# An interleaved two-layer decode kernel: w_down in 6272-byte runs, gate and up columns with a step of seven, the FFN result read once, new instruction orders

## The chip, the cores and the metric

One core of a Trainium2 chip. The metric is the device time of one execution in microseconds: 278.97 us, the median of three runs (278.21 to 281.98). TensorE (PE; its weight loads are PEld), VectorE (DVE), ScalarE (ACT) and GpSimd (POOL) compute; SyncE (SP) issues the transfers.

## What is computed

Four tokens (B = 4), each with a row x of 448 numbers, go through the same two blocks twice: attention over the last 2048 keys of a cache, and a gated FFN.

```python
x = A_x
x = x + _A_ref(_layernorm(x), ...)   # attention
x = x + _B_ref(_layernorm(x), ...)   # FFN
x = x + _A_ref(_layernorm(x), ...)   # the same weights and caches again
x = x + _B_ref(_layernorm(x), ...)

def _B_ref(x, w_gate, w_up, w_down):       # 448x1792, 448x1792, 1792x448
    g = _silu(x @ w_gate)
    return (g * (x @ w_up)) @ w_down
```

Attention has 16 query heads on 8 K/V heads of 256, bf16. K and V of the window are 64 MB for all tokens and heads in one layer; with weights and with what is loaded again for the second layer, some 96 MB are moved.

## The kernel before

**Tokens and heads.** A head of one token and layer is written t, layer, head: 301 is token 3, layer 0, head 1. `PLAN` lists the pairs of heads that are worked as one group, in 27 steps; a token's layer 1 (112, 113 and so on) is mixed with layer 0 of the next token. PLAN isn't changed.

**K and V slots.** Each K or V half (512 KB, 4096 bytes on each of 128 partitions) goes into one of 31 slots of the tile `half` (7 more are free once wq is done with). Part of a token's K and V stays for layer 1. SP issues the loads in the order `SEQ_SP`, with the slots of `SLOTS`; a load into a used slot waits for the matmul that read it last, and everything behind it in the queue waits too.

**A group.** DVE transposes each K half in place (L982, in blocks of 32). PE makes scores S (L1016), DVE the maximum (L1031), PE spreads it (L1036, L1039), DVE reduces again (L1045), ACT the exponent (L1049), PE turns the probabilities (L1060), ACT copies them (L1068), PE sums (L1076) and multiplies with V (L1090), DVE and POOL make the reciprocal (L1081, L1103), ACT and DVE take the result (L1105, L1107), PE flips it (L1113), DVE scales it (L1123), and PE projects it with wo into bank A, as rows (L1143) or columns (L1135).

**The FFN of a token in layer 0.** `rows` (L883 to L897) turns what is in rows; `residual` makes xn, the bf16 column form, early (L875), and xr in fp32 (L903). `norm` makes the odd part xe (L589, L592), the sums (L596, L599 with PE L602, DVE L609), and on POOL the inverse root (L615 to L625). Since the FFN starts ahead of the norm, the mean is put in afterwards with a matmul of the columns' sums (L629, L816). Gate and up are 14 x 4 matmuls each (L801): a 128x128 piece of the weights is loaded, and a column of xn, repeated to 32, streams through. Gate is in bank Z, up in bank Z2. ACT makes tanh (L832), DVE two products (L835, L846), then 56 matmuls with w_down (L853) put the result into bank Z again. That is for tokens 1 to 3; token 0's FFN comes after its mean is taken off (L607), and leaves the columns' sums (L843). In layer 1 there is one FFN for all four tokens at the end, with 8 columns for each.

**After it.** Three DVE operations (L870) read bank Z: `xn` (bf16, for the q projection), `xr` (fp32, for the norm), `xs` (fp32, kept for layer 1). Each is z * scale + old value. Then a norm (L589 to L623), the q projection (L683, into banks Z and Z2; it writes bank Z first, so it waits until Z was read), ACT and DVE copies (L694, L691), a turn (L703) with `tmean` (L665), L710, L717, L722, and the factor for the scores, `rid` (L650).

**The weights of the FFN.** Chunk fc of the hidden row has features 128 fc to 128 fc + 127. `w[:, cc * FF + fc * 128 : ... + 128]` is the piece for rows 128 cc of gate or up; the last 64 rows of w are folded into 128 partitions, half of the columns in each, so that chunk fc lies at (fc % 7) * 128 there. w_down is loaded (L576) with partition p of chunk c holding row 128 c + p, in rows of 896 bytes.

**Orders.** Every operation has a number, in the order in which the program makes them. `SEQ_PE`, `SEQ_DVE`, `SEQ_ACT`, `SEQ_POOL` and `SEQ_SP` say in which order each engine runs them. An engine runs in order, and waits at an operation for semaphores of other engines. `w` in `SEQ_PE` is a filler: a matmul of 128x128 by 512 that adds zero to bank A (L1253), to keep PE busy; there are 223. `HELD` says which fillers may come before a read of bank A.

Of the kernel before, what the change touches and what calls it, by code (L numbers as in the profile page):

```python
# [6 lines left out]
ALU = mybir.AluOpType  # L7
# [43 lines left out]
ROWF = ()  # L51
# [35 lines left out]
).split()  # L87
SEQ_DVE = (
# [18 lines left out]
).split()  # L107
SEQ_ACT = (
# [5 lines left out]
).split()  # L114
SEQ_POOL = (
# [8 lines left out]
).split()  # L124
SEQ_SP = (
# [13 lines left out]
).split()  # L139
HELD = (  # L140
    "0 44 44 44 94 94 99 99 115 115 119 122 139 139 145 145 195 195 201 201 208 208 213 213 215 215 215 215 215 215 "
    "215 215"
).split()
MMV = 0.034
FAR = 1e30
# [1184 lines left out]
```

## Time and profile before

| | |
|---|---|
| Runs | 278.97, 278.21, 281.98 us |
| The profiled execution | 279.5 us, its span from the first to the last instruction 277.7 |
| TensorE's mean granted clock | 0.969 |
| Busy | PE 209.0 us, weight loads 125.0, DVE 173.8, POOL 76.5, ACT 47.3 |
| Transfers | 96.68 MB, mean 348 GB/s, in 28474 packets, 6928 of them under 2 KB |
| FFN matmuls | 560 for gate and up, 280 for w_down |

A busy PE isn't PE at its peak, since matmuls are pipelined. In the chain of waits each piece is what the following one waited for. In a timeline a row is: start and length in us, engine, line, operation, tiles, count, and in brackets the idle time before it and what ended it. In a row of windows: the stretch, its length, busy us (and number of instructions) of PE, PEld, DVE, ACT and POOL, the granted clock, the busy share of the DMA engines (it can exceed 1), and GB/s.

### The profile page before, as it was taken

The page shows a single profiled execution, that of the slowest core. Times are in us where ns is not written, and L with a number is a line of the kernel's source. Part 1 is how long each engine was busy: PE and PEld are TensorE (multiplying, and loading weights), DVE is VectorE, ACT ScalarE, POOL GpSimd, SP SyncE. Part 2 cuts the span into 40 slices and gives each one's busy share as a digit, 9 for nine tenths or more (in the row PEclk, how much of TensorE's full clock was granted, in tenths as well). Part 3 has the DMA queues.
Part 4 walks back from the last instruction along what each step waited for, and adds up shares of the span by engine and source line. Part 5 has one row for each costly group of instructions (what it writes and reads, how often), then busy time and mean ns, then how long its engine had stood idle before and what let it go on. Part 6 is the DMA issues. An engine that isn't in the chain of part 4 may idle for free.

```text
span 277.7 us, 9966 instructions
## 1 busy us (share of the span) xinstructions
PE 209.0 (75%) x4424; PEld 125.0 (45%) x4424; DVE 173.8 (63%) x522; ACT 47.3 (17%) x115; POOL 76.5 (28%) x195
## 2 busy tenths in 40 slices
PE   0000076699788968988998897899699798899997
PEld 0000032355464634455754444474454356456694
DVE  7973056445545799368447995655789845559751
ACT  0000000232111220121113221211022031032510
POOL 1000017142204412421253342124132332043650
PEclk9999999999989999999999999999979999599998
DMA  7999999999999999999799999939999999589200
GB/s 292 394 419 412 403 412 406 402 396 401 389 379 405 357 396 415 407 409 353 260 332 410 409 405 411 405 150 362 362 417 407 410 408 346 215 279 408 79 5 1
DMA packets 28474, 96.68 MB, mean 348 GB/s; under 512 B 2828, under 2 KB 6928, under 8 KB 27792
## 3 DMA queue, kind: packets, MB, share of 16 engines
q1 hardware_dynamic: 28423, 96.06, 88.8%
q8 instruction: 34, 0.56, 0.8%
q14 instruction: 9, 0.07, 0.1%
q10 hardware_dynamic: 8, 0.00, 0.0%
HBM read 96.05 MB, written 0.00 MB: 346 GB/s over the span
## 4 chain that ended last, share of the span: by engine, by line
PE 43%; DMA 25%; DVE 13%; SPq 10%; issue 4%; ACT 3%; POOL 2%; ACTq 0%
DMA half<-in_A_k_cache_dram 16%; PE A L1253 10%; DMA half<-in_A_v_cache_dram 9%; PE S L1016 8%; DVE half L982 7%; PE Y L1090 6%; SPq L992 5%; PE Z L801 4%; SPq L976 3%; PE Z L683 3%; SPq L558 2%; PE Z L853 2%; PE A L1143 2%; PE Y L1060 2%; PE A L1135 2%
## 5 line engine op out<-in xcount | busy, mean ns | idle before, releaser
L982 DVE STREAM_TRANSPOSE half<-half 128x1024 uint32<-128x1024 uint32 x80 | 97.2, 1231 | 22.3 <-DMA half<-in_A_k_cache_dram 22.2
L1253 PE MATMUL A<-identb,small 128*128 128x512 bf16 x223 | 67.4, 404 | 0.3 <-DVE xr L903 0.3
L1103 POOL TENSOR_TENSOR small<-small 128x4 f32<-128x4 f32 x32 | 32.5, 1017 | 70.1 <-DVE small L1081 64.7
L1090 PE MATMUL Y<-half,pT 128*8 128x256 bf16 x1024 | 38.7, 275 | 3.2 <-issue 1.4
L1016 PE MATMUL S<-half,qe 128*8 128x256 bf16 (+1 forms) x1120 | 35.3, 269 | 6.3 <-issue 2.0
L1016 PEld LDWEIGHTS S<-half,qe 128*8 128x8 bf16 x1120 | 24.4, 84 | 16.2 <-issue 3.8
L1023 POOL TENSOR_TENSOR qe<-qc,small 128x64 bf16<-128x64 bf16 x56 | 15.3, 295 | 47.6 <-PE S L1016 33.9
L921 PE MATMUL Z<-identb,wo_sb 4*128 4x4 bf16 x4 | 0.3, 167 | 36.7 <-DMA wo_sb<-in_A_x_dram 36.7
L1031 DVE TENSOR_REDUCE small<-S 104x1 bf16<-104x256 f32 x32 | 13.4, 417 | 22.0 <-PE S L1016 22.0
L1090 PEld LDWEIGHTS Y<-half,pT 128*8 128x8 bf16 x1024 | 21.3, 85 | 12.0 <-DVE small L1081 3.2
L1253 PEld LDWEIGHTS A<-identb,small 128*128 128x128 bf16 x223 | 19.1, 103 | 14.9 <-issue 6.4
L1105 ACT ACTIVATE oh<-Y 128x256 bf16<-128x256 f32 x32 | 12.2, 383 | 36.2 <-PE Y L1090 27.2
L615 POOL TENSOR_SCALAR st<-st 128x1 f32<-128x1 f32 x16 | 4.5, 280 | 50.1 <-DVE st L609 50.1
L1107 DVE SCALAR_TENSOR_TENSOR oh<-oh,small,Y 128x256 bf16<-128x256 bf16 x32 | 15.0, 469 | 4.0 <-ACT oh L1105 3.8
L921 PEld LDWEIGHTS Z<-identb,wo_sb 4*128 4x128 bf16 x4 | 0.2, 104 | 36.6 <-DMA wo_sb<-in_A_x_dram 36.6
L1143 PE MATMUL A<-wo_sb,oT 128*4 128x448 bf16 x200 | 13.8, 352 | 1.3 <-DVE oT L1123 1.3
L1049 ACT ACTIVATE praw<-S,small 104x256 bf16<-104x256 f32 x16 | 7.6, 472 | 38.9 <-DVE small L1045 38.9
L1049 ACT ACTIVATE praw<-S,small,st 104x256 bf16<-104x256 f32 x16 | 9.0, 564 | 30.1 <-DVE small L1045 26.6
L1068 ACT ACTIVATE pT<-Y 128x192 bf16<-128x192 f32 x32 | 10.5, 329 | 15.5 <-PE Y L1060 14.1
L683 PE MATMUL Z<-half,small 128*5 128x512 bf16 x160 | 10.9, 379 | 1.5 <-DVE small L592 1.4
L1081 DVE TENSOR_REDUCE small<-Y 128x4 f32<-128x64 f32 x32 | 6.7, 213 | 7.8 <-PE Y L1076 7.6
L1060 PE MATMUL Y<-selt,praw 104*64 104x48 bf16 x256 | 10.1, 197 | 1.8 <-ACT praw L1049 1.7
(135 smaller groups left out, 245.8 us busy)
## 6 DMA issues: line engine op xcount, KB each, us to landing
half<-in_A_v_cache_dram SPq DMA_DIRECT2D x80, 512.0 KB, 13.5
half<-in_A_k_cache_dram SPq DMA_DIRECT2D x76, 512.0 KB, 10.7
wo_sb<-in_A_wo_dram SPq DMA_DIRECT2D x8, 448.0 KB, 11.8
half<-in_A_wq_dram SPq DMA_DIRECT2D x3, 1024.0 KB, 16.2
half<-in_A_k_cache_dram SPq DMA_DIRECT2D x2, 1024.0 KB, 6.4
wd_sb<-in_B_w_down_dram SPq DMA_DIRECT2D x1, 1568.0 KB, 18.5
wu_sb<-in_B_w_up_dram SPq DMA_DIRECT2D x1, 1344.0 KB, 11.8
wg_sb<-in_B_w_gate_dram SPq DMA_DIRECT2D x1, 1344.0 KB, 14.7
```

What stands on the lines that cost most here:

```text
L683: last = e.matmul(zb[32 * j:32 * j + B + 1, 0:512], lhsT=lhsT, rhs=wq_sb[:, c:c + 512], start=(cc == 0), stop=(cc == 3), skip_group_check= ...
L982: return e.transpose(a, a)
L992: g.dma(pp + VLAG, 1 << 19, lambda e, cell=cell, hv=hv, vsrc=vsrc: e.dma_start(unit(cell), vsrc[hv]), None, w=(f"v{t}_{kvh}_{hv}",), run=4 ...
L1016: last = e.matmul(Sb[s_][qd:qd + 8, c0:c0 + rhs.free_size()], lhsT=qe[q_][:, P, ce, :, :].rearrange("p a n -> p (a n)"), rhs=rhs, start=(c ...
L1023: g.op(*((DVE, 0.13) if layer and fresh.get(t, gi) == gi else (POOL, 0.25)), pos - SLEAD - 1, lambda e, P=P, t=t, kvh=kvh: e.tensor_tensor ...
L1049: return e.activation(praw[0:R, 0:128 * n].rearrange("p (g r l) -> p g r l", g=2 * n, l=2), Sb[s_][0:R, 0:128 * n].rearrange("p (l g r) -> ...
L1060: last = e.matmul(Yb[p_][64 * h:64 * h + 64, c0:c0 + (48 if n == 2 else 32)], lhsT=praw[0:R, 64 * gg:64 * gg + 64], rhs=w, start=(gg == 0) ...
L1090: last = e.matmul(Yb[p_][32 * gg:32 * gg + M, 256:512], lhsT=pT[pt][:, gg, 2 * a + hv, 4 * P:4 * P + M] if n == 2 else p1[:, gg % 2, 2 * a ...
L1103: g.op(POOL, 0.69, pos, lambda e: e.tensor_tensor(ri[p_][:, 0:2 * n], rs[p_][:, 0:2 * n], expo[:, 1:1 + 2 * n], op=ALU.pow), r=(f"rs{p_}", ...
L1107: g.op(DVE, 0.43, pos, lambda e: e.scalar_tensor_tensor(out=oh[:, :], in0=oh[:, :], scalar=lomask[:, 0:1], in1=Yb[p_][:, 256:512], op0=ALU ...
L1143: last = e.matmul(Ab[32 * k:32 * k + B, 0:D], lhsT=oT[oi][:, k % 2, k // 2, :], rhs=wo_sb[:, 4 * kvh + k, :], start=False, stop=False, ski ...
L1253: return e.matmul(Ab[:, 0:512], lhsT=zero[:, 0:1].broadcast_to([128, 128]), rhs=identb[:, :].unsqueeze(1).broadcast_to([128, 4, 128]), sta ...
```

## The change

**w_down.** Chunk fc = 7 h + j now has at partition p the feature 896 h + 7 p + j. Seven rows that follow each other lie in one partition, so a run is 7 x 896 = 6272 bytes, and two of them fill a partition. The gate and up pieces must yield the features in the same order: their 128 columns are every seventh one.

```diff
-            load(rank_d, 1605632, wd_sb[:, :, :], B_w_down.rearrange("(c p) n -> p c n", p=128), "wd", 430)
+            load(rank_d, 1605632, wd_sb[:, :, :].rearrange("p (h j) n -> p h (j n)", h=2),
+                 B_w_down.rearrange("(h p j) n -> p h (j n)", h=2, j=7), "wd", 6272)
...
                         if cc < 3:
-                            lhsT, x = w[:, cc * FF + fc * 128:cc * FF + fc * 128 + 128], xn[:, cc, sl]
+                            c, x = cc * FF + fc // 7 * 896 + fc % 7, xn[:, cc, sl]
                         else:
-                            lhsT = w[:, 3 * FF + (fc % 7) * 128:3 * FF + (fc % 7) * 128 + 128]
-                            x = xe[:, fc // 7, sl]
+                            c, x = 3 * FF + fc % 7, xe[:, fc // 7, sl]
+                        lhsT = w[:, c:c + 890:7]
```

**The FFN result.** One DVE operation reads bank Z and leaves z * scale in `st[:, t, 4:8]`. DVE adds it to xr for xn; POOL adds it to xr and to xs.

```diff
-            for dst, src, key, put in ((xn[:, :, t], xr[:, t, :], f"x{t}", f"xn{t}"), (xr[:, t, :], xr[:, t, :], f"x{t}", f"x{t}"),
-                                       (xs[:, t, :], xs[:, t, :], f"xs{t}", f"xs{t}")):
-                vec(rank, lambda e, dst=dst, src=src: e.scalar_tensor_tensor(
-                    out=dst, in0=zv[:, 0, :], scalar=st[:, t, 14:15], in1=src, op0=ALU.mult, op1=ALU.add),
-                    ("z", f"st{t}t", key), (put,), 0.1, ("Z",))
+            sk, d = f"st{t}", st[:, t, 4:8]
+            vec(rank, lambda e: e.tensor_single_scalar(d, zv[:, 0, :], st[:, t, 14:15], op=ALU.mult),
+                ("z", sk + "t"), (sk + "w", sk + "h"), 0.16, ("Z",))
+            vec(rank, lambda e: e.tensor_tensor(xn[:, :, t], xr[:, t, :], d, op=ALU.add), (f"x{t}", sk + "w"), (f"xn{t}",), 0.14)
+            for a, key in ((xr, f"x{t}"), (xs, f"xs{t}")):
+                g.op(POOL, 0.27, rank, lambda e, a=a: e.tensor_tensor(a[:, t, :], a[:, t, :], d, op=ALU.add),
+                     r=(key, sk + "w"), w=(key,))
```

The first two columns of `st[:, t, 4:8]` are scratch of the norm too, so the norm's L596 waits until POOL has read it.

**Orders.** All five orders, `SLOTS` and `HELD` are new. Each FFN of layer 0 has one operation more, so numbers from 304 on are up by one to four: an operation n of before is n + 1 after token 0's FFN, n + 2 after token 1's, n + 3 after token 2's and n + 4 after token 3's. There are 245 fillers. Two places, with the numbers as each version has them:

```diff
 SEQ_SP, around w_down (117; 115 and 113 are up and gate, 335 and 337 K 101, 437 K 102, 604 is K 200 and becomes 606)
-115 113 335 337 117 437 333 334 340 339
+115 113 338 336 606 117 335 334 341 340
 SEQ_DVE, the end of token 0's FFN (296 L846, 438 the transpose of K 102, 351 L1081, 301 to 303 L870; now 301 the read, 302 xn)
-296 344 346 438 303 351 301 302
+296 352 301 302
 SEQ_DVE, token 3's FFN (1263 and 1265 transposes of K 210, 1269 and 1271 of K 211; 1150 L875, 1151 L903, 1154 L596, 1153 L592, 1155 L599, 1157 L609, 1162 L629, 1174 L835, 1175 L846)
-1150 1151 1154 1153 1155 1157 1162 1271 1174 1269 1263 1265 1175
+1269 1153 1154 1157 1158 1156 1267 1160 1273 1165 1275 1177 1178
 SEQ_PE, token 1 after w_down (579 L589, 590 to 595 L683, 583 L602, 664 value products)
-579 590 591 583 592 664 594 595
+581 592 666 593 585 594
 SEQ_PE, token 3 (1163 to 1171 L801, 1167 and 1172 L816, 1156 L602, 1231 to 1234 value products of group 111, 1276 scores of 210 and 211, 1176 to 1179 L853)
-1231 1165 1168 1169 1166 1167 1232 1233 1170 1171 1172 w w w w w w 1276 1176 1177
+1166 1155 1167 1168 1169 1159 1237 w w w w w 1171 1172 1173 1174 1170 1175 1280 1179
```

The function `ffn_row`, and the branches that call it, are taken out; `ROWF` was empty and PLAN has no step of that kind, so nothing ran there.

More of the change, by code (lines that the diff above doesn't have):

```diff
@@ L50 @@
 DSTART = 2.1
-ROWF = ()
 COLX = {(3, 1): 2}
@@ L135 @@
     "0 1 2 3 4 5 6 7 8 9 10 11 12 13 14 15 16 17 18 19 20 21 22 23 24 25 26 27 28 29 30 3 4 19 21 22 14 20 9 7 10 21 "
[3 rows of a table removed]
[3 rows of a table added]
 ).split()
 HELD = (
-    "0 44 44 44 94 94 99 99 115 115 119 122 139 139 145 145 195 195 201 201 208 208 213 213 215 215 215 215 215 215 "
-    "215 215"
+    "0 45 45 45 110 110 113 113 131 131 133 133 151 151 160 160 220 220 224 224 231 231 237 237 237 237 237 237 237 "
+    "237 237 237"
 ).split()
@@ L724, in qproj @@
                     ("z2",), tuple(f"qc{t}_{h}" for h in range(HKV)), 0.18, ("Z2",))
-        def ffn_row(ts, rank):
-            rowvec(rvec[:, 1:2], "rvf", ts, rank)
-            g.op(POOL, 0.27, rank, lambda e: e.tensor_single_scalar(rvec[:, 2:3], rvec[:, 1:2], 0.5, op=ALU.mult),
-                 r=("rvf",), w=("rvs",))
-            g.op(POOL, 0.27, rank, lambda e: e.tensor_scalar(rvec[:, 3:4], rvec[:, 1:2], rvec[:, 2:3], None, op0=ALU.mult),
-                 r=("rvf", "rvs"), w=("rvt",))
-            def gu(e, gi, c0, c1):
-                last = None
-                w, zb = (wg_sb, wu_sb)[gi], (Zb, Z2)[gi]
-                for cc in range(c0, c1):
-                    for j in range(4):
-                        f0, f1 = 512 * j, min(512 * j + 512, FF)
-                        if cc < 3:
-                            parts = [(xn[:, cc, 0:B], cc * FF + f0, 0, f1 - f0)]
-                        else:
-                            parts = []
-                            for h in range(2):
-                                a, b = max(f0, 896 * h), min(f1, 896 * h + 896)
-                                if a < b:
-                                    parts.append((xe[:, h, 0:B], 3 * FF + a - 896 * h, a - f0, b - a))
-                        for lhsT, c, o, m in parts:
-                            last = e.matmul(zb[32 * j:32 * j + B, o:o + m], lhsT=lhsT, rhs=w[:, c:c + m],
-                                            start=(cc == 0), stop=(cc == 3), skip_group_check=True)
-                return last
-            for gi, (z, bank, w) in enumerate((("z", "Z", "wg"), ("z2", "Z2", "wu"))):
-                g.op(PE, 1.28, rank, lambda e, gi=gi: gu(e, gi, 0, 3), r=XN[0:B] + (w + "a",), w=(z,), bank=(bank,))
-                g.op(PE, 0.5, rank, lambda e, gi=gi: gu(e, gi, 3, 4), r=XE[0:B] + (w + "b",), acc=(z,), bank=(bank,))
-            g.op(SCA, 0.65, rank, lambda e: e.activation(wide[:, :], Zb[:, :], ACT.Tanh, scale=rvec[:, 2:3]),
-                 r=("z", "rvs"), w=WIDE, bank=("Z",))
-            vec(rank, lambda e: e.scalar_tensor_tensor(out=wide[:, :], in0=wide[:, :], scalar=1.0, in1=Zb[:, :],
-                                                       op0=ALU.add, op1=ALU.mult), ("z",), WIDE, 0.65, ("Z",))
-            vec(rank, lambda e: e.scalar_tensor_tensor(out=wideb[:, 0:512], in0=wide[:, :], scalar=rvec[:, 3:4], in1=Z2[:, :],
-                                                       op0=ALU.mult, op1=ALU.mult), ("z2", "rvt"), WIDE, 0.65, ("Z2",))
-            def turn(e):
-                last = None
-                for c in range(4):
-                    last = e.matmul(Zb[:, 16 * c:16 * c + 16].rearrange("p (j t) -> p j t", j=4),
-                                    lhsT=wideb[:, 128 * c:128 * c + 128], rhs=idt, start=(c == 0), stop=True,
-                                    skip_group_check=True)
-                return last
-            g.op(PE, 0.12, rank, turn, r=WIDE + ("identb",), w=("z",), bank=("Z",))
-            vec(rank, lambda e: e.tensor_copy(hT[:, :], Zb[:, 0:64]), ("z",), ("wb",), 0.13, ("Z",))
-            def down(e):
-                last = None
-                for c in range(4):
-                    for j in range(4):
-                        if 4 * j + c < NFC:
-                            last = e.matmul(Ab[32 * j:32 * j + B, 0:D], lhsT=hT[:, 16 * c + 4 * j:16 * c + 4 * j + 4],
-                                            rhs=wd_sb[:, 4 * j + c, :], start=False, stop=False, skip_group_check=True)
-                return last
-            g.op(PE, 1.5, rank, down, r=("wb", "wd"), acc=tuple(f"row{t}" for t in ts), bank=("A",))
@@ L1163, in build @@
             where = {}
-            if not heads:
-                g.tag = ("f", waiting[-1])
-                ffn_row(waiting, pos)
-                for u in waiting:
-                    rows(u, pos)
-                    residual(u, pos)
-                    final(u, pos)
-                g.tag = None
-                waiting = []
-                continue
             for batch in heads:
@@ L1222, in build @@
                 pos = pos_ - CROSS
-                with_ = []
-                rowf = t in ROWF and layer == 0
                 late = (t, layer) in LATE or layer == 1 and t in fin
                 residual(t, pos, late)
-                norm(t, pos, xr, None if rowf or (layer and not late) else fin.index(t) if layer else -1, late)
+                norm(t, pos, xr, None if layer and not late else fin.index(t) if layer else -1, late)
                 if layer == 0:
-                    if rowf:
-                        ffn_row(with_ + [t], pos)
-                        for u in with_ + [t]:
-                            rows(u, pos)
-                            residual(u, pos, u == t and t in QLATE)
-                        for u in with_:
-                            final(u, pos)
-                    else:
-                        ffn(with_ + [t], pos, late, False)
+                    ffn([t], pos, late, False)
                     norm(t, pos, xr, late=t in QLATE)
```

128 rows, old and new, of tables (SEQ_ACT, SEQ_DVE, SEQ_PE, SEQ_POOL) are left out of this document.

## Prediction

> **What bounds the kernel now.** I read the page first, then the chain of waits in order of time, then equal windows of the span, and last the timeline around each token's FFN.
>
> ```profile
> span 277.7 us, 9966 instructions
> ...
> GB/s 292 394 419 412 403 412 406 402 396 401 389 379 405 357 396 415 407 409 353 260 332 410 409 405 411 405 150 362 362 417 407 410 408 346 215 279 408 79 5 1
> ...
> PE 43%; DMA 25%; DVE 13%; SPq 10%; issue 4%; ACT 3%; POOL 2%; ACTq 0%
> ```
>
> Each of the 40 slices is 6.9 us. The loads run at about 405 GB/s for the first 85 us, and fall into four holes: slices 14, 19 to 21, 27 to 29 and 34 to 36. The last three each sit on the FFN of a token. The chain in order of time says the same from the other side:
>
> ```profile
> 64.60 18.34 DMA half<-in_A_k_cache_dram
> ...
> 95.00 12.57 DMA half<-in_A_k_cache_dram
> ...
> 238.82 2.56 PE A L1253 x6
> 241.38 1.44 PE S L1016 x29
> ```
>
> So the first 107 us are bound by the transfers, and the later part by what TensorE, VectorE and the slots do around an FFN: while an FFN runs, no K or V slot comes free, and the queue stands. The last FFN hole is the dearest:
>
> ```profile
> 235.00:240.00 5.00, 4.23 (x90) 2.58 (x87) 4.40 (x6) 0.27 (x1) 1.01 (x3) 0.54 0.65 210
> 240.00:245.00 5.00, 5.00 (x104) 2.92 (x102) 1.14 (x7) 0.61 (x2) 0.00 (x0) 0.77 0.53 197
> 245.00:250.00 5.00, 4.39 (x91) 2.28 (x90) 2.89 (x16) 1.81 (x4) 2.94 (x8) 1.00 0.93 320
> ```
>
> The last number is GB/s, the third from the end the granted clock. Against 410 GB/s these 15 us lack (200 + 213 + 90) x 5 us = 2.5 MB, or 6.1 us.
>
> **Part 1: w_down in long runs.** Transfers of 896-byte rows become 6272-byte runs.
>
> ```profile
> 70.00:74.00 4.00, 2.57 (x61) 1.48 (x59) 1.92 (x9) 0.93 (x2) 0.22 (x2) 1.00 1.03 408
> 75.00:79.00 4.00, 3.49 (x117) 3.22 (x116) 3.02 (x7) 0.27 (x1) 1.42 (x4) 0.57 1.09 347
> ...
> wd_sb<-in_B_w_down_dram SPq DMA_DIRECT2D x1, 1568.0 KB, 18.5
> ...
> 81.71 1.22 PE L853 MATMUL Z<-wide,wd_sb 128*128 128x32 bf16 x42 [0.52 <-DMA wd_sb<-in_B_w_down_dram]
> ```
>
> The down projection of token 0 waits for w_down until 81.7 us, so the window from 75 to 79 is mostly w_down, and the one from 70 to 74 is the gate matrix and K. 1568 KB are 1.606 MB: 4.63 us at 347 GB/s, 3.94 us at 408. That is 0.7 us of transfer time less. Ends: 0 if the time is lost again in the hole at 90 us, 1.0 us if the window still holds some long runs (estimate). [...]
>
> The queue is also reordered: one K half for token 2 (op 604, 512 KB, 1.28 us at 408 GB/s) now goes ahead of w_down. So w_down lands at 81.7 - 0.7 + 1.3 = 82.3. What follows it for token 0:
>
> ```profile
> 82.97 1.25 DVE L982 STREAM_TRANSPOSE half<-half 128x1024 uint32<-128x1024 uint32 x1 [1.55 <-DMA half<-in_A_k_cache_dram]
> 84.14 0.18 DVE L870 SCALAR_TENSOR_TENSOR xs<-Z,st,xs 128x4 f32<-128x4 f32 x1
> 84.37 0.21 DVE L870 SCALAR_TENSOR_TENSOR small<-Z,st,xr 128x4 bf16<-128x4 f32 x1
> 84.61 0.22 DVE L870 SCALAR_TENSOR_TENSOR xr<-Z,st,xr 128x4 f32<-128x4 f32 x1
> 84.89 0.39 PEld L683 LDWEIGHTS Z<-half,small 128*5 128x5 bf16 x12
> ```
>
> Before, a K transpose (op 438) stood on VectorE ahead of the three reads of bank Z, and held them until 84.14; the new order has it later. Now: 56 matmuls at 1.22 / 42 = 29 ns, with about 0.3 us of another group's turn between (estimate), end at 82.3 + 1.9 = 84.2; one read to 84.42, the bf16 row to 84.6, q projection at about 84.65 instead of 84.89. That gain of 0.25 us and the 0.7 us of transfers belong to the same chain (it goes back into the queue at 93 us and out by DMA at 95). I take 0.5 us for both.
>
> **Part 2: the FFN result read once.** Three VectorE operations that read bank Z become one read, one add on VectorE for bf16 xn, and two adds on GpSimd (xs first, then xr). Token 1 in the profile:
>
> ```profile
> 137.86 0.23 DVE L870 SCALAR_TENSOR_TENSOR small<-Z,st,xr 128x4 bf16<-128x4 f32 x1 [1.80 <-PE Z L853]
> 138.00 0.22 DVE L870 SCALAR_TENSOR_TENSOR xs<-Z,st,xs 128x4 f32<-128x4 f32 x1
> 138.13 0.22 DVE L870 SCALAR_TENSOR_TENSOR xr<-Z,st,xr 128x4 f32<-128x4 f32 x1
> 138.41 0.82 PE L683 MATMUL Z<-half,small 128*5 128x512 bf16 x12
> 139.16 0.38 PE L602 MATMUL Z<-st,small 128*128 128x2 f32 x2
> 139.58 0.16 DVE L609 COPY st<-Z 128x2 f32<-128x2 f32 x1 [0.79 <-PE Z L602]
> 139.84 0.30 POOL L615 TENSOR_SCALAR st<-st 128x1 f32<-128x1 f32 x1 [0.25 <-DVE st L609]
> 140.87 0.26 PE L703 MATMUL Z<-small,wide 128*128 128x4 bf16 x4
> ...
> L1245 POOL TENSOR_SCALAR xr<-xr,st 128x4 f32<-128x4 f32 x4 | 1.2, 311 | 7.4 <-DVE st L599 7.4
> ```
>
> The q projection overwrites bank Z, so it waited for all three reads (ending 138.35). Now: read to 138.08, xn 0.16 (as L609's) to 138.24, start near 138.29, 0.12 earlier. The norm goes the other way: its sums need xr, which was there at 138.35. GpSimd starts 0.10 after VectorE's end (139.74 to 139.84), takes 0.31 twice, and VectorE gets it 0.10 later, at 138.90: 0.5 us late. The norm's matmul L602 stands in TensorE's order in the middle of the q projection. For tokens 0 and 2 the new order puts more of it (and value products) ahead of L602, which covers the 0.5; for tokens 1 and 3 only 0.2 us more is put ahead, so TensorE stands some 0.3 us, and all behind L602 with it. Two new waits: GpSimd's adds wait for the read, and behind them stand the reciprocal of another group or the norm's own steps, which aren't due earlier; L596 waits on VectorE for the adds, and behind it stand the norm's steps, at token 2 also the softmax sum of group 301 (L1081), 0.5 us late at most. L703 (140.87) needs what follows L609, whose end goes from 139.74 to 140.24; that leaves 0.6 us for the one VectorE step between. Sum: token 0 counted above, token 1 +0.3, token 2 -0.2 (as token 1's start), token 3 +0.3, with ends of -0.25 and +0.5 for each of the three. I take +0.1 for tokens 1 and 2, and token 3 goes into part 4.
>
> **Part 3: columns with a step of seven.** 560 weight loads (112 for each of five FFNs, half of them the x280 below) read 128 columns 14 bytes apart.
>
> ```profile
> 75.63 1.30 PE L801 MATMUL Z<-small,wu_sb 128*128 128x32 bf16 x42
> ...
> 129.03 1.22 PE L801 MATMUL Z<-small,wg_sb 128*128 128x32 bf16 x42 [0.26 <-DVE small L875]
> ...
> L801 PE MATMUL Z<-small,wg_sb 128*128 128x32 bf16 x280 | 9.0, 180 | 0.3 <-DVE small L875 0.3
> ...
> L703 PE MATMUL Z<-small,wide 128*128 128x4 bf16 x32 | 2.0, 170 | 0.1
> ```
>
> Taking off one matmul's 0.18 us, 42 come every 25 ns at clock 1 and every 27 ns in the window with 0.57. Halving the clock hardly shows, so at the full clock the array's own share is at most 14 ns, and 25 ns is the interval of issue. Reads twice as slow would still fit (2 ns x 112 = 0.25 us per FFN). The nearest stepped weights, L703 with columns 4 bytes apart, come at (0.26 - 0.17) / 3 = 30 ns, like the plain ones. I take 0; the other end is the rival below.
>
> **Part 4: the orders.** PLAN is unchanged, so every group comes in the same place; what moves is the fine order. The largest move is at token 3:
>
> ```profile
> 178.12 1.46 PE L1253 MATMUL A<-identb,small 128*128 128x512 bf16 x6
> ...
> 232.83 0.17 DVE L875 TENSOR_TENSOR small<-xr,A 128x4 bf16<-128x4 f32 x1 [1.00 <-PE A L1135]
> 234.20 0.16 DVE L609 COPY st<-Z 128x2 f32<-128x2 f32 x1 [0.59 <-PE Z L602]
> 234.39 0.24 DVE L629 TENSOR_SCALAR wide<-colsum,st 128x28 bf16<-128x28 f32 x1
> 234.54 1.24 DVE L982 STREAM_TRANSPOSE half<-half 128x1024 uint32<-128x1024 uint32 x1
> 236.39 0.17 DVE L835 SCALAR_TENSOR_TENSOR wide<-wide,Z 128x14 f32<-128x14 f32 x1 [0.60 <-ACT wide L832]
> 236.47 3.49 DVE L982 STREAM_TRANSPOSE half<-half 128x1024 uint32<-128x1024 uint32 x3
> 239.88 0.13 DVE L846 TENSOR_TENSOR wide<-wide,Z 128x14 bf16<-128x14 f32 x1
> ```
>
> Three transposes stood between L835 and L846, and the scores of K 210 and 211 waited for them behind six fillers, 8.3 us after L875 ended (233.0 to 241.3). The new order puts one transpose ahead of L875, where TensorE's output projection runs anyway (1.00 us of idle time, so 0.25 is uncovered), and the others between L599, L609, L629 and L835. Counted from L875: VectorE four small steps like L875's 0.17, three transposes of 1.23, L609 0.16, L629 0.24, together 4.8 us; TensorE 112 x 25 ns = 2.8, the norm's matmul 0.38, 16 value products at the same interval 0.4, and five fillers. One filler takes (1.46 - 0.38) / 5 = 0.216 us, the six less the tail of the last, taken as L602's 0.38; five make 1.1, together 4.7. Scores start at 233.0 + 0.25 + 4.8 = 238.0 instead of 241.3, 3.3 us earlier; less 0.3 for L602, 3.0. Ends: 0 and 3.6. The loads that end the hole wait for these scores, so I carry it to the end.
>
> 22 fillers are added (223 to 245 in the orders). They stand mostly between token 0's late groups and before token 3's FFN. I take 0, since TensorE waits there for K and V; with the cover gone it is 22 x 0.216 = 4.8 us, and the six at 238.82 show that it can be gone.
>
> Sum: 279.5 us for the profiled execution (277.7 of span and 1.8 around it), less 0.5, plus 0.1, less 3.0: 276.1. The median of the runs shown is 0.5 below that execution: 275.5.
>
> **The rivals.** *The hole after token 3 closes (272.4).* Two value products of group 111 now come before and amid gate and up, which frees V slots earlier; if the queue never stands, 6.1 us of missing transfers come back in place of 3.0, and 3.1 less is 272.4. For it: the clock was 0.54 and 0.77 in those windows, and fillers there took 2.56 us for six; a busier TensorE may keep it at 1. Against: the loads behind still wait for the scores of 211.
>
> *The wait is only replaced (278.5).* VectorE works in order. If K 210 has not landed by 233 us, the transposes put ahead of L875 and L609 hold up the norm itself, and 3.0 goes back. For it: K is what the chain waits on elsewhere. Against: at 234.54 and 236.47 no transpose waited for a landing.
>
> *Stepped weight loads become the bound (288.8).* If reading 14 bytes apart takes the array four times as long, 14 ns become 55, 30 more than the issue interval: 112 x 30 = 3.3 us per FFN, four of them on the chain (token 0's has w_down's landing for cover): +13.3. It decides from a factor of about three. Nothing in the trace steps so far; L703's 4 bytes speak against. [...]
>
> **How the numbers follow.** Forecast 0.42 (own range 272.5 to 279, about 0.06 of it under 273.4), hole closes 0.24, wait replaced 0.18, weight loads 0.16. Two per cent of 278.97 is 5.6 us, about what a measurement of this kernel can tell from no change. Faster than 273.4: 0.24 + 0.06 = 0.30. Slower than 284.5: 0.16. The rest, 0.54, is within. Range 270.5 to 281: it leaves out the weight-load case and the lowest tip, and holds some uncovered fillers.
>
> **What would show it.** In the profile after: over 395 GB/s while w_down comes in, and 1792 - 256 = 1536 fewer packets; L801 x42 still near 1.2 us; bank Z read once, with L602 late by up to 0.5 us; at token 3 no transpose between L835 and L846, and scores within 5 us of L875; hole three narrower. The forecast is wrong if L801's interval grows past 30 ns, if transposes at token 3 show idle time ended by a K landing, or if the gain at 240 us is gone by the last FFN.

## The result, and the profile after

The changed kernel takes 302.38 us (300.41 to 303.88, six runs) where the one before takes 278.56 (277.49 to 281.98, six runs beside them): ratio 1.086, 95% interval 1.081 to 1.091. It is 23.8 us slower; the forecast was 275.5. The page of its profiled execution (302.5 us, of which 300.7 are span):

```profile
span 300.7 us, 9951 instructions
...
PE 235.4 (78%) x4414; PEld 143.6 (48%) x4414; DVE 175.1 (58%) x518; ACT 47.0 (16%) x115; POOL 77.5 (26%) x203
...
PEclk9999999999589999985799899969999997599957
...
GB/s 301 398 418 408 404 416 401 399 398 407 388 281 332 344 411 408 409 355 141 229 391 411 408 404 409 139 87 341 303 412 410 407 408 307 83 378 306 2 4 0
DMA packets 26937, 96.68 MB, mean 321 GB/s; under 512 B 2827, under 2 KB 5135, under 8 KB 26255
...
PE 52%; DMA 17%; DVE 14%; SPq 9%; ACT 3%; issue 2%; POOL 2%; ACTq 0%
```

Only TensorE changed: 26.4 us more of PE (209.0 before) and 18.6 more of weight loads (125.0), while VectorE, ScalarE and GpSimd are within 1.3 us. In the chain TensorE rose from 43 to 52% as the DMA fell from 25 to 17. PEclk dips around every FFN; in the kernel before its row was

```profile
PEclk9999999999989999999999999999979999599998
```

The operations that got longer stand in the groups by shape (busy us, mean ns of one, idle before) and in the timeline of token 1's FFN:

```profile
L746 PE MATMUL Z<-small,wg_sb 128*128 128x32 bf16 x280 | 16.5, 210 | 0.3 <-DVE small L822 0.3
L746 PEld LDWEIGHTS Z<-small,wg_sb 128*128 128x128 bf16 x280 | 16.1, 153 | 2.2 <-DVE small L822 0.8 <-issue 0.7 <-DVE st L596 0.4
...
L798 PE MATMUL Z<-wide,wd_sb 128*128 128x32 bf16 x280 | 8.4, 183 | 0.0
```

```profile
134.10 2.42 PE L746 MATMUL Z<-small,wg_sb 128*128 128x32 bf16 x42
...
138.38 1.44 PE L1180 MATMUL A<-identb,small 128*128 128x512 bf16 x3
139.61 3.15 PE L746 MATMUL Z<-small,wu_sb 128*128 128x32 bf16 x56
142.69 1.88 PE L963 MATMUL S<-half,qe 128*8 128x256 bf16 x32
```

L746 is the line of gate and up (L801 before). The gate product's busy time went from 9.0 to 16.5 us, while L798, the down product, which has the same shape and plain columns, stayed at 30 ns each. (2.42 - 0.18) / 41 is 55 ns where the same 42 matmuls came every 25 ns. From the start times of successive weight loads in the trace the median is 53 ns at full clock and 53 at half clock, against 25 and 27 before. Around them other work is slower too. The 32 score matmuls that follow took 1.08 us in the kernel before, at full clock, and now take 1.88:

```profile
133.95 1.08 PE L1016 MATMUL S<-half,qe 128*8 128x256 bf16 x32
```

The clock is at half there:

```profile
75.00:85.00 10.00, 9.98 (x153) 7.97 (x153) 4.75 (x12) 0.27 (x1) 1.42 (x4) 0.51 0.82 326
134.00:144.00 10.00, 10.00 (x152) 8.04 (x152) 3.93 (x8) 0.00 (x0) 1.42 (x4) 0.50 0.36 134
190.00:200.00 10.00, 9.74 (x164) 7.89 (x162) 3.61 (x12) 0.00 (x0) 1.51 (x6) 0.73 0.07 27
250.00:260.00 10.00, 9.74 (x142) 7.75 (x146) 4.61 (x13) 0.27 (x1) 1.42 (x4) 0.63 0.53 200
288.00:298.00 10.00, 10.00 (x180) 8.64 (x181) 1.94 (x13) 0.25 (x1) 1.79 (x5) 0.55 0.01 2
```

These are the windows of the five FFNs; the granted clock stands third from the end, GB/s last. Added over the trace, the clock is at half for 54.6 us (17.1 before), in stretches of 3.41, 6.83, 10.24 and 13.65 us. And while an FFN lasts longer, the queue stands longer: 134 and 27 GB/s at tokens 1 and 2, against 408 in a stretch without a hole. The lowest slices of the page there are 141 and 87 GB/s; before they were 260 and 150.

### The profile page after: what moved, and what is told of

Read it like the earlier page. It is cut to its first block, busy times and chain, and to the rows that moved or that the text cites. A ratio compares the mean times of both kernels' runs of the same rounds, so it can differ in the third digit from the quotient of the medians.

```text
span 300.7 us, 9951 instructions
## 1 busy us (share of the span) xinstructions
PE 235.4 (78%) x4414; PEld 143.6 (48%) x4414; DVE 175.1 (58%) x518; ACT 47.0 (16%) x115; POOL 77.5 (26%) x203
## 4 chain that ended last, share of the span: by engine, by line
PE 52%; DMA 17%; DVE 14%; SPq 9%; ACT 3%; issue 2%; POOL 2%; ACTq 0%
PE A L1180 11%; DMA half<-in_A_k_cache_dram 11%; PE Z L746 10%; PE S L963 7%; DVE half L929 7%; PE Y L1037 6%; DMA half<-in_A_v_cache_dram 6%; SPq L939 4%; PE A L1090 3%; PE Z L798 3%; PE Z L683 2%; SPq L923 2%; SPq L557 2%; PE A L1082 2%; PE Y L1007 2%
## 5 line engine op out<-in xcount | busy, mean ns | idle before, releaser
L1180 PE MATMUL A<-identb,small 128*128 128x512 bf16 x245 | 75.7, 411 | 0.3 <-DVE xr L850 0.3
L963 PE MATMUL S<-half,qe 128*8 128x256 bf16 (+1 forms) x1088 | 38.3, 289 | 2.9 <-DVE half L929 1.4
L978 DVE TENSOR_REDUCE small<-S 104x1 bf16<-104x256 f32 x32 | 13.3, 417 | 31.6 <-PE S L963 31.4
L1180 PEld LDWEIGHTS A<-identb,small 128*128 128x128 bf16 x245 | 21.1, 106 | 16.9 <-issue 8.6
L746 PEld LDWEIGHTS Z<-small,wg_sb 128*128 128x128 bf16 x280 | 16.1, 153 | 2.2 <-DVE small L822 0.8
L746 PE MATMUL Z<-small,wg_sb 128*128 128x32 bf16 x280 | 16.5, 210 | 0.3 <-DVE small L822 0.3
L746 PEld LDWEIGHTS Z<-small,wu_sb 128*128 128x128 bf16 x280 | 15.8, 153 | 1.5 <-issue 1.4
L746 PE MATMUL Z<-small,wu_sb 128*128 128x32 bf16 x280 | 15.8, 214 | 0.0
## 6 DMA issues: line engine op xcount, KB each, us to landing
wd_sb<-in_B_w_down_dram SPq DMA_DIRECT2D x1, 1568.0 KB, 17.6
```

The lines of the kernel that those rows point to most:

```text
L746: last = e.matmul((Zb, Z2)[gi][:, k * m * fc:k * m * fc + k * m], lhsT=lhsT, rhs=x.unsqueeze(2).broadcast_to([128, k, m]), start=(fc == 0 ...
L963: last = e.matmul(Sb[s_][qd:qd + 8, c0:c0 + rhs.free_size()], lhsT=qe[q_][:, P, ce, :, :].rearrange("p a n -> p (a n)"), rhs=rhs, start=(c ...
L978: g.op(DVE, (0.23, 0.36)[n - 1], pos, lambda e: e.tensor_reduce(pmax[s_][0:R, :], Sb[s_][0:R, 0:N], AX.X, ALU.max), r=(f"s{s_}",), w=(f"pm ...
L1180: return e.matmul(Ab[:, 0:512], lhsT=zero[:, 0:1].broadcast_to([128, 128]), rhs=identb[:, :].unsqueeze(1).broadcast_to([128, 4, 128]), sta ...
```

## The experiments

Two theories. S: the stepped weight loads cost it all, 28 ns for each of 560 directly and the rest by the clock that is lost while they run. O: the new orders, with 22 more fillers and GpSimd's adds, cost a good part. The first three runs separate them from both ends.

**Plain columns put back into the changed kernel.** The products pair columns with the wrong features (w_down keeps its long runs), so its output is another one.

```diff
-                            c, x = cc * FF + fc // 7 * 896 + fc % 7, xn[:, cc, sl]
+                            lhsT, x = w[:, cc * FF + fc * 128:cc * FF + fc * 128 + 128], xn[:, cc, sl]
...
-                        lhsT = w[:, c:c + 890:7]
```

> The changed kernel with its gate and up columns taken side by side again, all else as changed (so hidden features are paired with other rows of w_down than in the reference; the work is the same). Theory S (the stepped weight loads cost it: an interval of 53 ns for 25, 112 of them in each of five FFNs, and a lower clock through them): interval back to 25 ns, half-clock time from 44 us back to under 20, and 274 to 280 us. Rival O (the new orders, the 22 fillers and the waits for GpSimd cost it, the weight loads only fill waits): still over 290 us.

282.6 us (279.47 to 283.34) beside 278.33 of before, ratio 1.013 [1.005, 1.021]; interval 25 ns, 20.8 us at half clock (22.8 with what the clock's record holds past the last instruction; here and below only the span is counted). 19.8 of the 23.8 us are gone with the step, though the time is 2.6 us above the range of S.

**The step alone in the kernel before** (columns and features mispaired again; the edit is the reverse of the one above).

> The kernel before with columns seven apart in gate and up, and nothing else of the change (w_down keeps its rows, so features are paired otherwise than in the reference). S: 53 ns for 25, 3.1 us for each FFN, of which the first may hide under w_down's landing: 278.6 + 12 to 16 from the interval alone, 291 to 295, and up to 303 if the clock is lost as well. O: 278.6 + at most 3.

298.42 us (296.54 to 299.71), ratio 1.0725 [1.064, 1.081], 20.1 us more than before; interval 53 ns, 47.8 us at half clock. Both ends give the same price, so S holds for about 20 us, and a rest of about 1.2% is left for the other parts.

**Plain columns and w_down in rows of 896 bytes**, which is the changed kernel with parts 2 and 4 alone.

```diff
-            load(rank_d, 1605632, wd_sb[:, :, :].rearrange("p (h j) n -> p h (j n)", h=2),
-                 B_w_down.rearrange("(h p j) n -> p h (j n)", h=2, j=7), "wd", 6272)
+            load(rank_d, 1605632, wd_sb[:, :, :], B_w_down.rearrange("(c p) n -> p c n", p=128), "wd", 430)
```

> The changed kernel with plain columns and w_down in rows of 896 bytes: what is left is the FFN result read once and the orders. S: within 1 us of the run with plain columns and long runs, later by the 0.7 us that the long runs save if these are on the chain, 274.5 to 281. O: over 290 us. The prediction's parts 2 and 4 gave 2.9 us less than before, so 275.7 by them.

281.84 us, ratio 1.012 [1.005, 1.018], 28473 packets. Against 1.013 with long runs: the runs of w_down give no gain in time that can be seen. The prediction's parts 2 and 4 alone gave 275.7, so they miss by 6 us.

**A scan of steps.** The kernel before, with another step in each quarter of gate and up (another product). In the expectation T and P are two theories of the price: that it goes with the lines touched, 4 more for each step, or that only neighbours, read in pairs, are cheap.

```diff
+                        step = ((1, 2, 3, 4), (5, 6, 8, 7))[gi][cc]
+                        c, x = cc * FF + fc, xn[:, cc, sl] if cc < 3 else xe[:, fc // 7, sl]
...
+                        lhsT = w[:, c:c + 127 * step + 1:step]
```

> The kernel before, with the eight quarters of gate and up read in steps of 1, 2, 3, 4 (gate) and 5, 6, 8, 7 (up), so that the products of gate and up are others than the reference's. Only the interval of the weight loads is read from it. [...] Theory T (time by lines touched, 4 lines per step for 32 columns): a steady rise from 25 at a small step to 53 at 7 and 60 at 8. Theory P (two neighbours per read): 25 at step 1 and about 53 at all others; the step of 2 in L703 at 25 to 30 ns speaks against it.

The timeline at token 3; in order of the rows the steps are 1 and 2, then 3, then 5 and 6 (up), then 4 (gate's last quarter), then 8 and 7 (up):

```profile
239.66 0.85 PE L800 MATMUL Z<-small,wg_sb 128*128 128x32 bf16 x28
240.97 0.54 PE L800 MATMUL Z<-small,wg_sb 128*128 128x32 bf16 x14
241.36 1.37 PE L800 MATMUL Z<-small,wu_sb 128*128 128x32 bf16 x28
242.58 0.62 PE L800 MATMUL Z<-small,wg_sb 128*128 128x32 bf16 x14
244.38 1.78 PE L800 MATMUL Z<-small,wu_sb 128*128 128x32 bf16 x28
```

Less one matmul, (0.85 - 0.18) / 27 is 25 ns, (0.54 - 0.18) / 13 is 28, (0.62 - 0.18) / 13 is 34, (1.37 - 0.18) / 27 is 44. The medians over all five FFNs, by step: 25 ns at 1 and 2, 27 at 3, 34 at 4, 40 at 5, 47 at 6, 53 at 7, 60 at 8, the same at half clock but for 27 and 28 at steps 1 to 3. From 3 on it is a straight line of 6.6 ns for each step ((60 - 27) / 5), over a floor of 25 to 27 ns. So P falls: step 2 costs 25 ns as step 1 does, and steps 3 to 6 lie between 27 and 47. The rise to 53 at 7 and 60 at 8 is what T expected.

**A second scan, to tell lines from distance.** As above, with 8, 9, 10 and 6 in gate, 11, 12, 14 and 5 in up.

> The kernel before with wider steps between the columns that one gate or up weight load takes: 8, 9, 10 and 6 in the four quarters of the gate product, 11, 12, 14 and 5 in those of the up product (columns and features are mispaired, so the product is another one). From the first scan: 40 ns at step 5, 47 at 6, 60 at 8. If a load's time goes with the 16-byte lines that its columns touch (eight bf16 to a line): every column has a line of its own from step 8 on, so 60 ns at 8, 9, 10, 11, 12 and 14 alike. If it goes with the distance spanned: 6.7 ns for each further step, 67, 73, 80, 87 and 100 ns at 9, 10, 11, 12 and 14.

Medians: 60 ns at 8 and 9, 57 to 58 at 10 and 11, 58 to 59 at 12, 60 at 14, 47 at 6, 40 at 5. It stays flat at 57 to 60 from 8 on, where the columns are 16 bytes or more apart; by the distance it would have been 67 to 100 from 9 on. Of the two theories in the expectation the one with lines of 16 bytes fits, to 3 ns. That is a fit to the intervals of two scans; the lines themselves no trace shows.

**Is the clock lost because the array is too little busy?** The changed kernel with one more filler behind each of the 40 quarters of gate and up, then with three.

```diff
 SEQ_PE (token 0)
-284 288 289 290 291 285 286 344 287
+284 w 288 w 289 w 290 w 291 w 285 w 286 w 344 287 w
```

> The changed kernel, step of seven and all, with one more filler matmul (512 columns) behind each of the 40 quarters of the gate and up products of the five FFNs. The weight-load interval stays 53 ns in any theory. If the clock is lost because the array itself is too little busy while loads come every 53 ns: the time at half clock falls from 54.6 us to under 25, and the time is 302.4 + 40 x 0.216 less the 4.4 us that the lost clock cost = about 307. If the clock falls for another reason: half-clock time stays near 50 us, and the fillers cost 40 x 0.216 to 40 x 0.45, 311 to 320.

306.09 us (305.2 to 307.16), as expected; half clock 37.5 us within the span (39.6 with what the record holds past it), which is less than 54.6 but not under 25. The 40 fillers at 0.216 us each are 8.6 us, but the time grew by only 3.7. The mean clock of its runs is 0.939 to 0.955, of the changed kernel's 0.909 to 0.926. With one filler it was not decided, so the same with three (the 0.0133 us in its expectation is an estimate; by the fillers it is 0.216 x 32 / 512 = 0.0135, which leaves its shares within one point):

> The changed kernel, step of seven and all, with three more filler matmuls behind each of the 40 quarters instead of one. Counting as the array's own work 0.0133 us for a matmul of 32 columns (at full clock, 0.216 us for 512) and 53 ns for each weight load, an FFN keeps the array 25% busy in the changed kernel, 42% with one filler for each quarter, 60% with three; the kernel before has 53%. If it is this share that the granted clock follows: half-clock time falls from 39.6 us (one filler) to about before's 17, at most 25. If it is the spaced weight loads or something else around an FFN: it stays at 35 to 55 us. The time grows in both: 80 fillers more than with one, 80 x 0.216 = 17 us at full clock, less up to 3 us of the clock's; about 320 against 325 or more.

320.18 us and 17.1 us at half clock, as much as before the change, with the weight loads as far apart as ever. Windows of token 2's FFN in the changed kernel (above, 190 to 200), with one filler, and with three:

```profile
189.00:199.00 10.00, 9.74 (x128) 7.63 (x127) 3.30 (x11) 0.00 (x0) 1.48 (x5) 0.83 0.32 127
```

```profile
195.00:210.00 15.00, 14.56 (x198) 10.23 (x195) 4.54 (x16) 0.27 (x1) 1.53 (x6) 1.00 0.22 84
```

0.73, 0.83, 1.00: here the granted clock rose with the array's own work. Over the whole span the half-clock time was 54.6 us, 37.5 with one filler and 17.1 with three, always with 53 ns between the loads; that is what the expectation gave for a clock that follows the array's share of work. How much work holds the clock, and over what time, these runs don't show. The column PE shows nothing of it, with 9.74 of 10 us "busy" at 0.73: the rows of the gate product are 210 ns long where they were 180 before, with the loads 28 ns further apart.

**Part 2 alone:** the kernel before with the FFN's result read once, GpSimd's adds where the changed kernel has them in its order.

```diff
-            for dst, src, key, put in ((xn[:, :, t], xr[:, t, :], f"x{t}", f"xn{t}"), ...
...
+            vec(rank, lambda e: e.tensor_single_scalar(d, zv[:, 0, :], st[:, t, 14:15], op=ALU.mult),
...
+            vec(rank, lambda e: e.tensor_tensor(xn[:, :, t], xr[:, t, :], d, op=ALU.add), ...
+            for a, key in ((xr, f"x{t}"), (xs, f"xs{t}")):
+                g.op(POOL, 0.27, rank, lambda e, a=a: e.tensor_tensor(a[:, t, :], a[:, t, :], d, op=ALU.add),
...
```

> The kernel before with the FFN result read once (product in st, cast on VectorE, the two adds on GpSimd) and nothing else: columns, w_down and all other orders as before, the adds put into GpSimd's order at the places that the changed kernel gives them. The prediction's part 2: +0.1 us (ends -0.5 and +0.6), so 278.4 beside 278.3, ratio 0.998 to 1.003. Rival, that GpSimd's adds and the longer way to the first norm step carry what the changed kernel with plain columns lies above the one before (3.5 to 4.3 us): 281.8 to 282.6, ratio 1.012 or more. Between the two, 279.5 to 281, it would be a part of it.

280.08 us beside 279.77, ratio 1.001 [0.996, 1.007]: nothing. VectorE's rows at token 1:

```profile
140.68 0.22 DVE L869 TENSOR_SCALAR st<-Z,st 128x4 f32<-128x4 f32 x1 [1.81 <-PE Z L853]
140.94 0.17 DVE L871 TENSOR_TENSOR small<-xr,st 128x4 bf16<-128x4 f32 x1
...
141.42 0.17 DVE L596 SCALAR_TENSOR_TENSOR st<-xr,small 128x4 f32<-128x4 f32 x1 [0.19 <-POOL xr L873]
...
142.45 0.16 DVE L609 COPY st<-Z 128x2 f32<-128x2 f32 x1 [0.65 <-PE Z L602]
```

From the read of Z to L609 it takes 1.77 us, before 1.72 (137.86 to 139.58).

**19 fillers fewer.** The run with plain columns and rows, without the fillers that stand between a down projection and the end of the q projection behind it (7, 2, 8 and 2 for tokens 0 to 3).

```diff
 SEQ_PE (token 2)
-905 906 955 w w 922 957 923 911 959 w 924 915 w w 926 929 960 927 961 962 930 w w w 966 932
+905 906 955 922 957 923 911 959 924 915 926 929 960 927 961 962 930 966 932
```

> The changed kernel with plain columns and w_down in rows of 896 bytes, as in the run before of that name, and without the 19 filler matmuls that stand between the last part of a down projection and the last step of the q projection behind it (7, 2, 8 and 2 for tokens 0 to 3); nothing else moves. If those fillers lie uncovered on the path: 19 x 0.216 = 4.1 us less, 277.7, ratio to before 0.998. If they only fill waits: 281.8, ratio 1.012. If they hold the clock: more time at half clock than the 12.4 and 22.8 us of the two plain-column profiles, and a longer time, 283 or more.

279.85 us (277.72 to 285.4, twelve runs), ratio 1.003 [0.998, 1.007], 17.1 us at half clock. This lies between the 0.998 and the 1.012 that were expected, 0.9% or 2.5 us under the ratio with them. The two intervals overlap ([0.998, 1.007] and [1.005, 1.018]), so the size is loose; it is best read as fillers that lay partly on the path, at some 0.13 us each.

**Token 3's VectorE order alone,** in the kernel before:

```diff
 SEQ_DVE
-1145 1147 1140 1142 1143 1150 1151 1154 1153 1155 1157 1162 1271 1174 1269 1263 1265 1175 1277
+1145 1140 1147 1142 1143 1265 1150 1151 1154 1155 1153 1263 1157 1269 1162 1271 1174 1175 1277
...
```

> The kernel before with one thing of the new orders: VectorE's order around token 3's FFN (the steps and transposes from token 3's residual to its q projection) as in the changed kernel, so that no transpose stands between the SwiGLU's two last steps; nothing else moves. The prediction's part 4: the scores start at about 238.0 instead of 241.3 and 3.0 us of it are kept to the end, 275.3 beside 278.3, ratio 0.989. Rival 'the wait is only replaced': token 3's stage gets shorter but what follows waits for the same K and V transfers, 278.3 within 0.6, ratio 0.998 to 1.002. What the changed kernel with plain columns showed (token 3's gate to down 5.7 instead of 9.7 us, no gain at the end) speaks for the rival.

290.23 us, ratio 1.0425 [1.0355, 1.0495]. Slower than either theory said, and this row tells of the larger wait (K half 210's transpose, now ahead of L875):

```profile
236.67 1.25 DVE L982 STREAM_TRANSPOSE half<-half 128x1024 uint32<-128x1024 uint32 x1 [6.60 <-DMA half<-in_A_k_cache_dram]
237.84 0.13 DVE L875 TENSOR_TENSOR small<-xr,A 128x4 bf16<-128x4 f32 x1
```

VectorE stands 6.6 us before a transfer that SP's order brings later, and the FFN stands behind it: L875 ends at 237.97, before at 233.0. These 5 us are about half of the loss. The time at half clock is 34.1 us instead of 17.1 as well; no run takes the two apart. The order of one engine can't be taken from the change alone; this run prices a wait, not part 4.

**Long runs with a small step.** The kernel before with w_down in runs of three rows (2688 bytes; six of seven chunks) and a step of three.

```diff
+                    out.append(e.dma_start(wd_sb[:, 7 * h:7 * h + 6, :].rearrange("p (a i) n -> p a (i n)", i=3),
+                                           B_w_down[896 * h:896 * h + 768, :].rearrange("(a p i) n -> p a (i n)", p=128, i=3)))
...
+                        c, s = (384 * (i // 3) + i % 3, 3) if i < 6 else (768, 1)
...
+                        lhsT = w[:, c:c + 127 * s + 1:s]
```

> The kernel before with w_down in longer runs alone, but with a step of three: each half's 896 rows as two times 128 runs of three rows (2688 bytes) and 128 single rows, in four transfers, and the gate and up columns of six of seven chunks with a step of three; all orders as before. From the scan: 27 ns instead of 25 for 96 of 112 weight loads, +0.2 us per FFN. The prediction's part 1 (-0.7, ends 0 and -1.0) on top: about 278.4 beside before's 278.5 to 279.8, ratio 0.996 to 1.002, interval 27 ns, clock as before. If any step at all costs the clock (rival): over 30 us at half clock and ratio 1.02 or more.

279.03 us beside 279.75, ratio 0.997 [0.994, 1.001], interval 26 ns. It has the lowest ratio of all these runs, 8% under the changed kernel's, but is not to be told from the one before.

## Why the prediction was wrong

**The failed step is part 3**, "25 ns is the interval of issue. Reads twice as slow would still fit ... I take 0": a cost put at nothing measures some 20 us. The bound of 14 ns for the array's own share was a bound on work that scales with the clock, as the fillers do (six take 1.46 us at 178.12, at full clock, and 2.56 at 238.82, at half). The read of stepped weights doesn't: with a step of seven it takes 53 ns at either clock, and in the scans its time goes with the step up to 8 and no further (27 ns at 3, 60 at 8, 57 to 60 to 14). At step 1 nothing of it shows in the 25 ns, and no row of before could tell how far under it lies. L703, the row that I let speak against the rival, has a step of two, which the scan finds free (25 ns). The rival "stepped weight loads become the bound", at 0.16, was what happened: it had 55 ns for the interval (53 measured) and 288.8 us for the time, and the sign that it named, an interval past 30 ns, showed. It missed two things. All five FFNs pay, token 0's too, since the loads (76.2 to 84.0 us) end after w_down's landing: 28 ns x 560 is 15.7 us, not 13.3. And the clock is lost around each FFN (0.50 to 0.73 in the five windows). The rest up to 20, some 4 us, is put down to it by difference; that the first fillers cost 3.7 us instead of 8.6 fits, but no run takes the clock alone.

**Part 1** was right about the transfer; its gain in time is too small to be told. w_down comes in at full rate, as these windows of the changed kernel show:

```profile
75.00:79.00 4.00, 3.98 (x58) 3.38 (x58) 3.03 (x8) 0.00 (x0) 1.42 (x4) 0.52 1.02 406
79.00:82.00 3.00, 3.00 (x61) 2.81 (x63) 0.94 (x1) 0.00 (x0) 0.00 (x0) 0.50 0.99 402
```

406 GB/s (347 before; over 395 forecast), and 1537 packets fewer (1536 forecast). Its landing, 17.6 us behind the issue at 64.2, is at 81.8, before at 81.7, with one more K half ahead of it (82.3 forecast). The two runs with plain columns have the same queue order: in rows w_down lands at 82.7 (65.2 + 17.5), in long runs at 81.7 (64.2 + 17.5), a microsecond sooner, though it was also issued that much sooner. In the kernel's time neither that pair (1.012 and 1.013) nor the step of three (0.997 [0.994, 1.001]) shows a gain. The 0.5 taken is inside what can't be told.

**Part 2** was taken at +0.1 and measured at 1.001 [0.996, 1.007]. Its inner terms were too dear: GpSimd's adds take 0.20 us each, not 0.31, and L609 at token 1 is 0.05 late, not 0.5.

**Part 4** was right at its place and wrong about the rest of the path. With plain columns and rows the chain at token 3 reads:

```profile
235.88 0.18 DVE small L821
...
239.41 1.39 PE Z L745 x56
240.81 0.05 PE Z L760 x2
240.85 1.03 PE S L962 x30
```

L821 is before's L875. Scores start 240.85 - 236.06 = 4.8 us behind its end, where 5.0 was forecast and 8.3 were before, and gate to the end of down takes 7.3 us (236.10 to 243.38) instead of 11.3 (233.10 to 244.42). But L875's counterpart ends at 236.06 instead of 233.0: 3.1 us were lost on the way. The windows of before, then of this run, say where:

```profile
185.00:195.00 10.00, 9.45 (x214) 5.55 (x206) 5.39 (x24) 2.06 (x5) 3.33 (x9) 1.00 0.78 299
195.00:205.00 10.00, 7.80 (x162) 4.46 (x154) 6.60 (x11) 1.68 (x4) 2.55 (x7) 0.83 0.98 385
205.00:215.00 10.00, 9.78 (x188) 5.01 (x177) 9.97 (x19) 2.85 (x7) 2.69 (x5) 1.00 1.03 409
```

```profile
185.00:195.00 10.00, 9.47 (x204) 5.27 (x201) 3.05 (x15) 2.06 (x5) 3.00 (x7) 1.00 0.69 251
195.00:205.00 10.00, 8.68 (x188) 4.92 (x191) 8.45 (x19) 1.68 (x4) 2.79 (x11) 1.00 0.93 321
205.00:215.00 10.00, 8.52 (x167) 4.51 (x155) 9.07 (x18) 1.95 (x5) 3.26 (x7) 1.00 1.02 411
```

Behind token 2's FFN the queue moved (299 + 385 - 251 - 321) x 10 us = 1.1 MB less, 2.7 us at 410 GB/s, and from 205 to 235 both run at about the full rate, so it can't be made up ahead of token 3. The chain of this run then waits for the queue, where that of before stood on VectorE and TensorE:

```profile
210.27 16.23 DMA half<-in_A_v_cache_dram
```

At token 3 itself the hole in the queue did get narrower, as forecast. The windows of before, then of this run:

```profile
235.00:245.00 10.00, 9.23 (x192) 5.50 (x188) 5.54 (x12) 0.88 (x3) 1.01 (x3) 0.66 0.59 203
245.00:255.00 10.00, 8.84 (x202) 5.35 (x205) 7.89 (x25) 2.70 (x6) 4.42 (x13) 1.00 0.97 365
```

```profile
235.00:245.00 10.00, 9.74 (x260) 7.01 (x260) 7.22 (x23) 1.22 (x3) 2.04 (x8) 1.00 0.86 324
245.00:255.00 10.00, 8.68 (x200) 5.21 (x196) 7.63 (x21) 2.36 (x5) 4.35 (x13) 1.00 1.01 390
```

That is (324 + 390 - 203 - 365) x 10 us = 1.5 MB more, which makes up the 1.1 MB, and still the end came no earlier: from the end of token 3's down projection to the gate product of the last FFN it takes 25.1 us, before 23.8, and that product starts at 268.48, before at 268.18. So the step "The loads that end the hole wait for these scores, so I carry it to the end" failed as well: the loads came sooner, but the chains of both runs from 243 to 268 us show no transfer, only work of TensorE, VectorE and ScalarE.

One thing on the path ahead of token 3 is the q projection of token 2: 4.4 us from its first to its last row with the new orders, with three fillers amid it where before had none, 2.8 before, and still 4.0 without those fillers. So "22 fillers ... I take 0" failed too: the 19 taken out (not the very 22 that were added) cost some 2.5 us by the two ratios, between 0 and the 4.1 of the price without cover, 0.216 each. The rest of the loss before token 3, with other things of the new orders in it, is read from the traces; no run took it apart, since slots, SP's order and the engines' orders hang together (as the run with VectorE's order alone showed).

Added up: step of seven +20 us, fillers about +2.5, all else about 0 (the run without 19 fillers: 1.003 [0.998, 1.007]), against the 23.8 measured. The difference is within the intervals. (The forecast's own sum, 276.1 less 0.5, is 275.6 and not 275.5; nothing hangs on that.)

## What to carry to other kernels

A stepped read can be hidden until it takes longer than what it hides under: here steps 1 and 2 both showed 25 ns, and step 7 showed 53. A bound from the clock's halving says nothing of a cost that doesn't scale with the clock (53 ns at full and at half), so a row of the same step, or one run that changes the step alone, has to stand in for it. If a layout wants long runs and columns in between, choose the step by its measured price: a step of three bf16 columns cost 2 ns and no time that could be seen (ratio 0.997), seven doubled the interval (25 to 53 ns). And when one stage gets faster, look at whether the transfers arrive earlier at its start: the 4 us gained in token 3's FFN were given back before and behind it, and the transfers that it then let in sooner were no longer what the end waited for.

## What the hardware showed that was not expected

A weight load of 128 stepped bf16 columns took 6.6 ns more for each step from 3 to 8 (27 to 60 ns), then stayed at 57 to 60 ns to step 14, at full and at half clock alike. And slow weight loads cost twice: with 53 ns between loads the granted clock was at half for 54.6 us of 300.7 (17.1 of 277.7 before); three fillers of 512 columns in each quarter brought that to 17.1, at the price of a longer time, 320.18 us.
